# Another order of the attention's events in a fused attention, soft-MoE and MLP kernel

## The chip, the cores and the metric

The kernel runs on one core of one Trainium2 chip. Its time is the device time of one execution in microseconds (us). Five engines work side by side, each through its own list of instructions and strictly in the order of that list: TensorE (PE, with its weight loads as PEld), VectorE (DVE), ScalarE (ACT), GpSimd (POOL) and SyncE (SP), which in this kernel issues every DMA. An instruction that needs a result of another engine waits at the head of its list, and everything behind it waits too.

## The reference, cut to what matters

```python
def _attn_ref(q, k, v, g_q, g_k):             # q, k, v: (4, 12, 448, 64), float32
    def rmsnorm(x, g):
        rms = np.sqrt(np.mean(x * x, axis=-1, keepdims=True) + 1e-06)
        return x / rms * g
    q_n, k_n = (rmsnorm(q, g_q), rmsnorm(k, g_k))
    scores = np.matmul(q_n, k_n.transpose(0, 1, 3, 2)) / np.sqrt(64)
    scores = scores - np.max(scores, axis=-1, keepdims=True)
    attn = np.exp(scores)
    attn = attn / (np.sum(attn, axis=-1, keepdims=True) + 1e-09)
    return np.matmul(attn, v).astype(np.float32)

def _moe_ref(x, phi, w1, w2):                 # x: (1792, 768), 8 experts of 4 slots
    logits = x @ phi
    d = softmax(logits, axis=0);  slot_input = d.T @ x
    slot_out[e] = np.maximum(slot_input[e] @ w1[e], 0.0) @ w2[e]
    c = softmax(logits, axis=1);  return c @ slot_out

def _moe2_ref(x, w_in, w_out, alpha):         # d_model 768, d_ff 2048
    h = x @ w_in
    g = np.maximum(h, 0.0) + alpha * np.minimum(h, 0.0)
    return g @ w_out
```

The three follow each other. (The two softmax lines of the soft-MoE are shortened; a softmax there subtracts the maximum and divides by the sum plus 1e-9.) `w_in` and `w_out` arrive as float64 and are narrowed to float32 on the chip.

## The kernel before

**The attention.** The 48 heads are taken in 24 pairs of two heads; a pair has 2 x 448 = 896 rows, seven tiles of 128. Two pairs form a group, which is loaded together (`load_qk`, eight DMAs, L605 and L611; `load_v`, L601 and L611). A pair goes through these steps:

- ScalarE squares q and k (`norm_sum`, L641), VectorE sums the squares (L643); for a group, `norm_rs` makes the factors 1/rms (L653 to L663).
- GpSimd multiplies (L684), ScalarE and GpSimd split into a high and a low half in fp16 (L690, L697), TensorE transposes (`turn`, L710), ScalarE copies the result into the tiles q and k (`turned`, L717) and SyncE copies halves of them into the tiles kB and qB (L719, L721) and within q (`twin`, L726).
- TensorE computes rough scores (`rowmax_mm`, L760), VectorE takes their row maxima (`rowmax`, L769), TensorE transposes these (`turn_m`, L731), ScalarE copies them into `mr` (L737), and SyncE puts `mr` into a row of qB (L738).
- TensorE computes the scores exactly in two passes over the same PSUM bank (`score_mm`, L778): q times k, and then kB times qB. The second pass brings the missing products and, through the row that came from `mr`, the subtraction of the row maximum. So this pass cannot start before the DMA of L738 has landed.
- ScalarE takes the exponential (`score`, L792 to L799), VectorE or GpSimd makes its low half (`score_lo`, L810), TensorE multiplies by v (`av`, eight groups to a pair, L827 and L837), and VectorE divides by the sum (`av_out`, L852 to L865).

Between these steps run three background queues: `bg`, the soft-MoE's logits and its two softmaxes, batch by batch (L899 to L1011); `pf`, which fetches w_in and the first expert weights in pieces (`fetch_in`, L488, 512 KB; `fetch` with a cut of 6, L479, 256 KB); and `cv`, which narrows w_in (L502 to L514).

PSUM has two banks for exact scores (`psn`), three for rough ones (`psr`), one for the product with v (`psv`) and two for transposes (`pst`).

**What sets the order.** `plan` lists 2374 such events, each a function and its arguments. The table `ORDER` names them in the order in which they are called, and since scheduling is manual, each engine gets its instructions in just this order. Table `T` gives positions that build the list and settings that choose engines; it is the same in both kernels. SyncE's DMAs take eight semaphores in turn, so that each also waits for the DMA eight places before it.

**Behind the attention.** When the last pair's tiles are free, three rings of buffers open (`close_norm`, `close_score`, `close_exp`) and take expert weights: 11 units of 1.5 MB in all, six of them in pieces. The last batch's dispatch softmax follows, the experts (L1285 to L1314), for which each unit's buffer is filled again as soon as TensorE has read it, and then the two products of the MLP (L1459 to L1461), blocked over tokens. The load of alpha (L1195) stands in SyncE's list behind the eleventh unit and ahead of the twelfth; its buffer is free once the last batch's combine weights (L1011) are done. None of this is ordered by the table.

```python
        assert sorted(ORDER) == list(range(len(plan)))
        plan = [plan[i] for i in ORDER]
        ...
        for _, f, args in plan:
            f(*args)
            while waiting and waiting[0][1]():
                waiting.pop(0)[0]()
```

Of the kernel before, what the change touches and what calls it, by code (L numbers as in the profile page):

```python
# [232 lines left out]
    1775, 968, 992, 1076, 920, 969, 993, 1016, 932, 1028, 1040, 1052, 1064, 1100, 1148, 1124, 921, 1796, 970, 994,  # L233
    1172, 1797, 971, 995, 1196, 1244, 1220, 1077, 1101, 840, 850, 860, 870, 880, 890, 1268, 900, 910, 944, 1292, 1316,
    72, 192, 1149, 1125, 312, 96, 432, 1017, 216, 336, 552, 456, 1986, 2171, 576, 672, 696, 1173, 956, 933, 2172, 792,
    1340, 1798, 1197, 1245, 1029, 1041, 1269, 1221, 1293, 1053, 1065, 1317, 1078, 1102, 1126, 816, 1364, 1150, 1198,
    73, 193, 313, 97, 217, 337, 1246, 1174, 1222, 433, 1079, 1388, 457, 553, 577, 673, 1270, 1294, 945, 972, 996, 793,
    1127, 697, 817, 1341, 1318, 1103, 74, 1175, 973, 1151, 1365, 1412, 1413, 2173, 2174, 1389, 1799, 194, 841, 997,
    851, 1223, 314, 861, 871, 881, 891, 98, 218, 1018, 1030, 1800, 0, 24, 2175, 1987, 120, 1042, 1054, 1066, 1199,
    144, 168, 1801, 1080, 338, 1104, 1128, 901, 911, 240, 1247, 1295, 264, 288, 1152, 360, 384, 1436, 408, 1176, 48,  # L240
    957, 1776, 1988, 2176, 434, 554, 1200, 480, 674, 458, 578, 698, 1989, 1224, 600, 794, 504, 624, 528, 1802, 1803,
    720, 744, 648, 1508, 768, 1081, 1342, 1105, 1319, 1437, 1580, 1778, 1271, 2177, 1, 1556, 2178, 121, 1532, 25, 145,
    75, 818, 1366, 195, 1390, 99, 219, 169, 241, 265, 2179, 1804, 2180, 315, 1628, 1990, 1652, 1676, 435, 2181, 974,
    1991, 1129, 1805, 1153, 361, 385, 409, 339, 998, 975, 1604, 1700, 1724, 1248, 555, 675, 842, 852, 862, 872, 882,
    289, 892, 481, 49, 902, 459, 912, 505, 601, 529, 1992, 1748, 1177, 1225, 625, 1806, 2182, 1201, 1807, 1296, 579,
    1993, 721, 745, 649, 769, 795, 1343, 1509, 1994, 1995, 1581, 1272, 1320, 1808, 2183, 2184, 2, 26, 2185, 699, 819,
    1533, 122, 1809, 1810, 999, 1460, 1414, 1438, 146, 1811, 1812, 1813, 1629, 1082, 1996, 1997, 1814, 170, 1019,
    1031, 1043, 2186, 242, 2187, 1055, 1067, 2188, 50, 266, 1815, 1653, 1367, 1391, 1677, 1816, 1817, 362, 1557, 1605,
    922, 1484, 934, 1106, 1130, 290, 76, 386, 410, 1998, 482, 602, 1701, 1725, 1749, 1154, 196, 316, 100, 220, 946,
    506, 626, 976, 958, 1249, 722, 746, 340, 1297, 1321, 650, 530, 436, 2189, 460, 556, 1818, 580, 2190, 770, 1273,  # L250
    2191, 676, 1510, 1202, 796, 1178, 1226, 1083, 1558, 700, 820, 3, 1461, 1819, 1415, 1000, 27, 2192, 77, 197, 977,
    101, 221, 317, 341, 1630, 1792, 123, 243, 147, 1107, 843, 267, 51, 853, 1534, 1001, 1777, 1131, 171, 1368, 1344,
    291, 1820, 1392, 2193, 863, 1821, 1155, 1822, 437, 1582, 1439, 873, 883, 893, 1654, 903, 913, 2194, 1606, 2195,
    363, 387, 1678, 483, 1702, 1726, 1823, 1824, 1825, 1485, 461, 1826, 1250, 1750, 603, 557, 677, 507, 531, 1416,
    2196, 627, 723, 747, 1274, 1020, 1440, 1827, 1298, 581, 651, 701, 411, 771, 1511, 1322, 1999, 1559, 797, 1583,
    1203, 4, 28, 821, 2000, 2001, 1032, 1044, 1631, 1056, 1068, 1179, 124, 1828, 78, 198, 2197, 148, 102, 1535, 172,
    244, 1462, 2002, 2003, 1655, 268, 222, 318, 292, 2198, 52, 1679, 1227, 364, 978, 1084, 438, 1607, 923, 2199, 2200,
    2201, 1345, 388, 484, 508, 412, 558, 1780, 1829, 1486, 1830, 1831, 1108, 1703, 1727, 1832, 342, 1369, 1393, 604,
    724, 1132, 935, 2004, 628, 748, 1251, 1751, 532, 1299, 1323, 947, 772, 652, 1833, 1793, 678, 462, 582, 702, 1156,
    1512, 1204, 1275, 959, 1560, 1536, 1417, 798, 1002, 1584, 5, 2202, 1632, 29, 1180, 2005, 1441, 1834, 822, 53, 125,  # L260
    149, 2203, 79, 245, 1463, 1346, 979, 173, 199, 319, 269, 1487, 1228, 1085, 1109, 844, 103, 854, 223, 1608, 1656,
    343, 1680, 864, 1704, 1728, 2204, 293, 1779, 2205, 365, 439, 463, 389, 2206, 1157, 1835, 1370, 559, 1133, 2207,
    1836, 1837, 1205, 1394, 1752, 485, 509, 605, 629, 1181, 1003, 874, 884, 894, 1838, 904, 914, 1252, 1418, 653, 725,
    2208, 1276, 679, 799, 749, 2006, 1442, 1300, 413, 2209, 533, 1324, 773, 1513, 1585, 2007, 1561, 6, 126, 583, 703,
    823, 1464, 1839, 30, 1840, 150, 80, 1537, 2210, 246, 174, 270, 104, 200, 224, 54, 1229, 1609, 1086, 1347, 2211,
    2008, 2212, 366, 2009, 2010, 390, 1371, 1841, 1488, 1395, 414, 1842, 1633, 980, 2011, 320, 1657, 344, 294, 440,
# [1284 lines left out]
```

## Time and profile before

| what | us |
|---|---|
| median of 3 runs | 696.68 |
| the runs | 689.49 to 698.57 |
| the profiled execution | 698.2 |
| its span, first to last instruction | 696.2 |
| PE busy | 618.2 |
| DVE busy | 472.7 |
| ACT busy | 364.5 |
| POOL busy | 192.6 |
| mean granted TensorE clock | 0.967 |

The profile is of one execution. Busy time is the time in which an engine works on an instruction; the shares over the whole span are means over stages with different limits, so they are read stage by stage. In lists of waits, a wait for several results is put down to the one that came last by the profile, and that can be the wrong one where two land together. PSUM tiles carry the names psn, psr, psv and pst; DMA issues of SyncE are shown as SPq.

### The profile page before, as it was taken

What the parts mean: (1) busy time and instruction counts of PE and PEld (TensorE: products, weight loads), DVE (VectorE), ACT (ScalarE), POOL (GpSimd) and SP (SyncE); (2) the same over time, 40 slices, a digit from 0 to 9 for tenths busy, and PEclk for the clock granted to TensorE, in tenths of its full rate; (3) what the DMA queues carried; (4) which work ended last, traced back from release to release, by engine and by line L of the source; (5) the groups of instructions that cost most, each with busy time, mean ns of one, the idle gap of its engine ahead of it and who ended that gap; (6) DMA issues with size and microseconds to landing.
All of it is one profiled execution on the core that took longest, in us unless ns stands there. A gap on an engine that the chain in (4) does not pass through costs nothing.

```text
span 696.2 us, 14030 instructions
## 1 busy us (share of the span) xinstructions
PE 618.2 (89%) x5522; PEld 479.6 (69%) x5522; DVE 472.7 (68%) x967; ACT 364.5 (52%) x708; POOL 192.6 (28%) x200
## 2 busy tenths in 40 slices
PE   0799898898889999998998657899999999999997
PEld 0367665576656766775543213787899999999997
DVE  5788997899999999864311042999975545454541
ACT  2799996898898997772111121766531111111110
POOL 5976665466647654321101000000000000000000
PEclk9889999999999999998899979999999999999999
DMA  5477666644735622759799999250020101010101
GB/s 138 109 209 197 174 161 190 178 118 115 191 93 154 180 50 61 211 164 399 313 422 425 425 423 425 107 182 1 1 91 0 47 1 46 1 45 1 47 1 45
DMA packets 65425, 106.90 MB, mean 154 GB/s; under 512 B 34632, under 2 KB 51536, under 8 KB 61008
## 3 DMA queue, kind: packets, MB, share of 16 engines
q1 hardware_dynamic: 65360, 106.01, 45.6%
q8 instruction: 43, 0.70, 0.4%
q14 instruction: 22, 0.18, 0.1%
HBM read 92.18 MB, written 5.51 MB: 140 GB/s over the span
## 4 chain that ended last, share of the span: by engine, by line
PE 50%; DVE 23%; DMA 12%; ACT 8%; issue 3%; SPq 2%; POOL 2%; ACTq 0%; DVEq 0%; POOLq 0%
PE psa L1461 9%; PE psa L1460 9%; PE psa L1459 9%; DMA unit<-in_moe_w_dram 8%; DVE m L769 4%; PE psn L778 4%; PE psv L837 3%; PE psv L827 3%; PE psa L1285 2%; DVE e L810 2%; PE psr L760 2%; DVE wf L510 1%; ACT e L794 1%; PE psa L1314 1%; PE pst L1416 1%
## 5 line engine op out<-in xcount | busy, mean ns | idle before, releaser
L1459 PE MATMUL psa<-whi,gh 128*128 128x384 f32 (+1 forms) x448 | 152.7, 341 | 0.0
L1460 PE MATMUL psa<-wlo,gh 128*128 128x384 f32 (+1 forms) x448 | 151.8, 339 | 0.0
L1461 PE MATMUL psa<-whi,gl 128*128 128x384 f32 (+1 forms) x448 | 151.4, 338 | 0.0
L769 DVE TENSOR_REDUCE m<-psr 128x1 f16<-128x448 f32 x168 | 97.2, 615 | 5.9 <-PE psr L760 5.4
L1428 ACT CAST gh<-t 128x512 fp32r<-128x512 f32 x40 | 24.9, 622 | 123.0 <-DVE t L1425 122.5
L1461 PEld LDWEIGHTS psa<-whi,gl 128*128 128x128 f32 x448 | 84.7, 189 | 3.0 <-DVE gl L1408 0.2
L1460 PEld LDWEIGHTS psa<-wlo,gh 128*128 128x128 f32 x448 | 84.7, 189 | 2.8
L837 PE MATMUL psv<-vH,e 128*128 128x65 f16 (+1 forms) x1152 | 85.7, 195 | 1.0 <-DVE e L810 0.9
L1459 PEld LDWEIGHTS psa<-whi,gh 128*128 128x128 f32 x448 | 84.7, 189 | 2.6
L837 PEld LDWEIGHTS <-e 128*128 128x128 f16 (+1 forms) x1728 | 80.8, 106 | 1.5 <-DVE e L810 1.2
L1422 DVE TENSOR_SCALAR t<-pst,alpha_t 128x256 f32<-128x256 f32 x80 | 34.9, 476 | 61.9 <-PE pst L1416 61.9
L810 POOL TENSOR_TENSOR e<-ef,e 128x448 f16<-128x448 f32 x48 | 53.7, 1119 | 83.1 <-ACT ef L799 65.4
L827 PEld LDWEIGHTS psv<-vR,e 128*128 128x128 f32 (+1 forms) x384 | 59.6, 178 | 22.9 <-issue 10.9
L837 PE MATMUL psv<-vL,e 128*128 128x64 f16 (+1 forms) x576 | 73.7, 193 | 0.1
L794 ACT ACTIVATE e<-psn 128x448 f16<-128x448 f32 x120 | 65.1, 542 | 14.2 <-PE psn L778 11.1
L778 PE MATMUL psn<-q,k 128*128 128x448 f16 (+1 forms) x192 | 62.5, 368 | 11.0 <-DVE e L810 4.9
L827 PE MATMUL psv<-vR,e 128*128 128x65 f32 (+1 forms) x384 | 69.9, 264 | 1.9 <-DVE X L865 0.7
L760 PE MATMUL psr<-k,q 128*128 128x448 f16 (+1 forms) x192 | 58.8, 378 | 6.8 <-DVE m L769 4.0
L778 PE MATMUL psn<-qB,kB 67*128 67x448 f16 (+1 forms) x192 | 62.2, 364 | 2.8 <-DMA vR<-in_v_dram 2.8
L697 POOL TENSOR_TENSOR sp<-nf,sp 128x448 f16<-128x448 f32 x48 | 51.2, 1076 | 13.9 <-ACT sp L690 11.0
L810 DVE TENSOR_TENSOR e<-psn,e 128x448 f16<-128x448 f32 x72 | 44.2, 616 | 9.3 <-ACT psn L799 8.8
L710 PE MATMUL pst<-ident,sp 128*128 128x128 f16 x336 | 28.4, 233 | 19.2 <-POOL sp L697 19.0
(164 smaller groups left out, 1077.4 us busy)
## 6 DMA issues: line engine op xcount, KB each, us to landing
unit<-in_moe_w_dram SPq DMA_DIRECT2D x26, 1536.0 KB
unit<-in_moe_w_in_dram SPq DMA_DIRECT2D x24, 512.0 KB
rawo<-in_moe_w_out_dram SPq DMA_DIRECT2D x8, 1536.0 KB
unit<-in_moe_w_dram SPq DMA_DIRECT2D x36, 256.0 KB
out_dram<-osb SPq DMA_DIRECT2D x14, 384.0 KB
qk<-in_q_dram SPq DMA_DIRECT2D x24, 192.0 KB
qk<-in_k_dram SPq DMA_DIRECT2D x24, 192.0 KB
vR<-in_v_dram SPq DMA_DIRECT2D x48, 96.0 KB
```

The source lines that it names most:

```text
L697: eng.tensor_tensor(out=d["sp"][:, a, :, D:], in0=d["nf"][:, a], in1=d["sp"][:, a, :, 0:D], op=ALU.subtract)
L760: nc.tensor.matmul(pn[o0:o1, :S], d["q"][:, c0 : c0 + o1 - o0], d["k"][:, h * S : (h + 1) * S], start=True, stop=True)
L769: nc.vector.tensor_reduce(out=d["m"][:, c : c + 1], in_=d.pop(("pn", c))[:, :S], axis=AX.X, op=ALU.max)
L778: nc.tensor.matmul(pe[o0:o1, :S], lhs[:, c0 : c0 + o1 - o0], rhs[:, h * S : (h + 1) * S], start=st_, stop=not st_,)
L794: nc.scalar.activation(e2[:, 0], pe[:, :S], AF.Exp, scale=0.125)
L810: eng.tensor_tensor(out=e2[:, 1], in0=ef, in1=e2[:, 0], op=ALU.subtract)
L827: nc.tensor.matmul(pv[o0:o1, slot, :], d["e", c][:, qs], d["vv"][:, sl], start=(j == 0), stop=False,)
L837: nc.tensor.matmul(pv[o0:o1, slot, 0:wd], d["e", c][:, w // 2, qs], (vl if w == 1 else vh)[:, sl, 0:wd], start=(j == 0 and w == 0), stop=( ...
L1422: nc.vector.tensor_scalar(out=t0[:, cs], in0=ph[:, cs], scalar1=0.0, scalar2=alpha_t[:, f // 2, i : i + 1], op0=ALU.min, op1=ALU.mult)
L1459: nc.tensor.matmul(a, gh[f][:, ms], hi[:, hs], start=(f == 0 and not (packed and m % 2 == 1 and hf == 0)), stop=False)
L1460: nc.tensor.matmul(a, gh[f][:, ms], lo[:, hs], start=False, stop=False)
L1461: nc.tensor.matmul(a, gl[f][:, ms], hi[:, hs], start=False, stop=(f == KF - 1 and not (packed and m % 2 == 0 and hf == 1)))
```

## The change

The numbers of `ORDER` are replaced by another arrangement of the same 2374 numbers; they were searched for offline, with longer DMA times and random changes of the durations. Nothing else differs: each engine has the same instructions, tiles and engine choices. One line of the table before and after:

```diff
 ORDER = (
-    1775, 968, 992, 1076, 920, 969, 993, 1016, 932, 1028, 1040, 1052, 1064, 1100, 1148, 1124, 921, 1796, 970, 994,
+    1076, 968, 1775, 992, 969, 993, 1016, 921, 1028, 1040, 1052, 1064, 920, 1100, 1124, 1986, 1148, 1196, 1244, 2171,
 ...
```

**SyncE, between the scores of pair 6 and pair 7.** These are the loads of k for pairs 12 and 13 (qk), the copies of pair 8's halves (qB2, kB2), two pieces of w_in and of w1 (unit), and the row maxima of pair 7 (qB1<-mr). Before:

```order
L605 DMA qk_1531<-in_k_dram 128x2x192
L611 DMA qk_1531<-in_k_dram 64x2x64
L605 DMA qk_1531<-in_k_dram 128x2x192
L611 DMA qk_1531<-in_k_dram 64x2x64
L721 DMA qB2_118<-q_1641 64x896
L488 DMA unit_1493<-in_moe2_w_in_dram 128x1024
L719 DMA kB2_119<-k_1664 64x896
L488 DMA unit_1493<-in_moe2_w_in_dram 128x1024
L726 DMA q_1438<-q_1438 64x896
L479 DMA unit_1760<-in_moe_w1_dram 128x512 x3
L738 DMA qB1_116<-mr_1778 1x7x128
L479 DMA unit_1760<-in_moe_w1_dram 128x512
```

Now:

```order
L605 DMA qk_1525<-in_k_dram 128x2x192
L721 DMA qB2_118<-q_1648 64x896
L611 DMA qk_1525<-in_k_dram 64x2x64
L605 DMA qk_1525<-in_k_dram 128x2x192
L719 DMA kB2_119<-k_1670 64x896
L611 DMA qk_1525<-in_k_dram 64x2x64
L726 DMA q_1437<-q_1437 64x896
L488 DMA unit_1485<-in_moe2_w_in_dram 128x1024 x2
L738 DMA qB1_116<-mr_1784 1x7x128
L479 DMA unit_1814<-in_moe_w1_dram 128x512 x2
L601 DMA vR0_122<-in_v_dram 128x3x64 x2
```

The three pieces of w1 have moved from ahead of pair 7's row maxima to behind them, and the copies of pair 8 have moved in between the loads of k, so that the last load of k stands behind the copy of pair 8's k.

**ScalarE, from pair 8's k to the square of pair 12** (sqr reads what the loads above bring). Before:

```order
L717 COPY k_1664<-pst16_1654 128x896
L792 ACTIVATE e2_1714<-psn_1700 128x448
L794 ACTIVATE e2_1716<-psn_1703 128x448
L799 ACTIVATE psn_1703<-psn_1703 128x448
L502 ACTIVATE win0_1073<-unit_655 128x768
L794 ACTIVATE e2_1736<-psn_1732 128x448
L799 ACTIVATE psn_1732<-psn_1732 128x448
L794 ACTIVATE e2_1770<-psn_1763 128x448
L799 ACTIVATE ef_1772<-psn_1763 128x448
L883 COPY xT_1776<-pst_1709 128x448
L737 CAST mr_1778<-pst_1774 7x128
L641 ACTIVATE sqr_1793<-qk_1531 128x896
```

Now:

```order
L717 COPY k_1670<-pst16_1618 128x896
L792 ACTIVATE e2_1691<-psn_1688 128x448
L794 ACTIVATE e2_1719<-psn_1704 128x448
L799 ACTIVATE psn_1704<-psn_1704 128x448
L794 ACTIVATE e2_1722<-psn_1713 128x448
L799 ACTIVATE psn_1713<-psn_1713 128x448
L502 ACTIVATE win0_1089<-unit_783 128x768
L794 ACTIVATE e2_1751<-psn_1743 128x448
L799 ACTIVATE ef_1753<-psn_1743 128x448
L883 COPY xT_1762<-pst_1708 128x448
L737 CAST mr_1784<-pst_1738 7x128
L641 ACTIVATE sqr_1830<-qk_1525 128x896
```

The same ten kinds of instruction stand between the two ends; one narrowing step (L502) has moved back by two exponentials. What changed is that the square's load now follows the DMA that reads the k at the top.

**VectorE, at the start, from the second group's square sums to its factors** (u and y; m are row maxima of pair 0). Before:

```order
L643 TENSOR_REDUCE u_221<-sqr_222 128x2x7
L643 TENSOR_REDUCE u_221<-sqr_226 128x2x7
L769 TENSOR_REDUCE m_276<-psr_268 128x1
L769 TENSOR_REDUCE m_276<-psr_270 128x1
L769 TENSOR_REDUCE m_276<-psr_274 128x1
L769 TENSOR_REDUCE m_276<-psr_278 128x1
L769 TENSOR_REDUCE m_276<-psr_287 128x1
L769 TENSOR_REDUCE m_276<-psr_291 128x1
L656 TENSOR_SCALAR u_221<-u_221 128x28
L659 TENSOR_TENSOR t_282<-y_281 128x28
L661 TENSOR_TENSOR t_282<-t_282,u_221 128x28
L663 SCALAR_TENSOR_TENSOR y_281<-t_282,y_281 128x28
```

Now:

```order
L643 TENSOR_REDUCE u_231<-sqr_232 128x2x7
L769 TENSOR_REDUCE m_257<-psr_252 128x1
L769 TENSOR_REDUCE m_257<-psr_254 128x1
L769 TENSOR_REDUCE m_257<-psr_263 128x1
L769 TENSOR_REDUCE m_257<-psr_266 128x1
L643 TENSOR_REDUCE u_231<-sqr_270 128x2x7
L656 TENSOR_SCALAR u_231<-u_231 128x28
L659 TENSOR_TENSOR t_278<-y_277 128x28
L661 TENSOR_TENSOR t_278<-t_278,u_231 128x28
L663 SCALAR_TENSOR_TENSOR y_277<-t_278,y_277 128x28
```

Two row maxima have moved behind the factors, and one of the two square sums has moved behind four row maxima.

Behind the last rough-score matmul (L760) TensorE's list now holds 32 instead of 28 exact-score matmuls and 24 instead of 22 groups of the product with v.

## Rows read from the trace of the kernel before

**Rows 1.** The page's first line: the span and the number of instructions

```profile
span 696.2 us, 14030 instructions
```

**Rows 2.** Busy us (count) by engine in each stretch, granted clock, DMA share, GB/s

```profile
core 0: us, PE busy (x) PEld busy (x) DVE busy (x) ACT busy (x) POOL busy (x), PEclk, DMA share, GB/s
0.00:60.00 60.00, 36.69 (x338) 23.31 (x339) 42.83 (x104) 41.88 (x81) 43.94 (x54) 0.91 0.62 163
60.00:300.00 240.00, 218.06 (x2757) 159.70 (x2755) 226.90 (x471) 208.62 (x425) 137.32 (x129) 0.98 0.54 144
300.00:322.00 22.00, 21.19 (x310) 16.92 (x308) 11.10 (x31) 14.22 (x32) 4.17 (x5) 1.00 0.76 265
322.00:337.00 15.00, 12.38 (x94) 8.16 (x95) 7.09 (x25) 1.39 (x5) 0.91 (x2) 0.66 0.85 356
337.00:440.00 103.00, 78.16 (x600) 31.67 (x591) 25.46 (x68) 22.96 (x42) 6.27 (x13) 0.95 0.95 398
440.00:696.30 256.30, 251.73 (x1440) 239.82 (x1438) 159.36 (x273) 75.47 (x127) 0.00 (x0) 0.99 0.11 41
```

**Rows 3.** SyncE's queue: waiter, releaser, us in total, times, longest

```profile
SPq L1195 <- DVE cN L1011: 15.4, 1, 15.4
```

**Rows 4.** VectorE's waits from 60 to 300 us, largest first

```profile
DVE e L810 <- ACT psn L799: 5.0, 7, 1.8
DVE m L769 <- PE psr L760: 1.5, 1, 1.5
DVE z L852 <- PE psv L837: 1.3, 1, 1.3
```

**Rows 5.** TensorE in order of time: start us, us, form [idle before, releaser]

```profile
107.98 0.35 PE L778 MATMUL psn<-q,k 128*128 128x448 f16 x1 [0.43 <-ACT ef L799]
111.11 0.46 PE L778 MATMUL psn<-qB,kB 67*128 67x448 f16 x1 [2.79 <-DMA vR<-in_v_dram]
```

**Rows 6.** SyncE's DMA issues in order of time, in front of the pause

```profile
102.92 1.56 SPq L479 DMA_DIRECT2D unit<-in_moe_w_dram  x3
104.57 0.80 SPq L738 DMA_DIRECT2D qB<-mr  x1
```

**Rows 7.** Three short stretches with half clock, columns as in rows 2

```profile
110.00:116.00 6.00, 4.89 (x53) 4.51 (x54) 2.88 (x5) 1.91 (x5) 4.52 (x6) 0.72 0.77 208
132.00:140.00 8.00, 6.68 (x79) 3.88 (x79) 6.37 (x19) 4.80 (x11) 2.97 (x4) 0.79 0.40 90
268.00:276.00 8.00, 6.51 (x63) 3.96 (x62) 6.59 (x15) 5.30 (x12) 2.99 (x3) 0.79 0.03 7
```

**Rows 8.** VectorE in order of time, behind the pause

```profile
113.77 0.63 DVE L769 TENSOR_REDUCE m<-psr 128x1 f16<-128x448 f32 x1 [1.52 <-PE psr L760]
116.17 0.62 DVE L810 TENSOR_TENSOR e<-psn,e 128x448 f16<-128x448 f32 x1 [1.77 <-ACT psn L799]
```

**Rows 9.** The chain that ended last, 102 to 112 us: start us, us, what

```profile
103.00 0.37 PE psv L827 x2
103.37 0.27 PE psv L837 x9
104.99 0.87 PE psn L778 x4
```

**Rows 10.** ScalarE in order of time: pair 8's k, squares of pairs 12 and 16

```profile
98.91 0.88 ACT L717 COPY k<-pst 128x896 f16<-128x896 f16 x1
104.33 0.94 ACT L641 ACTIVATE sqr<-qk 128x896 f32<-128x896 f32 x1
158.18 0.95 ACT L641 ACTIVATE sqr<-qk 128x896 f32<-128x896 f32 x1 [2.01 <-DMA qk<-in_k_dram]
```

**Rows 11.** SyncE's issue of pair 16's last load

```profile
153.23 0.60 SPq L611 DMA_DIRECT2D qk<-in_k_dram  x1
```

**Rows 12.** The stretch of pair 16's wait, columns as in rows 2

```profile
155.00:160.00 5.00, 5.00 (x89) 4.38 (x88) 4.93 (x15) 2.99 (x7) 1.12 (x1) 1.00 0.83 247
```

**Rows 13.** GpSimd in order of time at the start

```profile
25.79 0.94 POOL L684 TENSOR_TENSOR nf<-qk,y 128x448 f32<-128x448 f32 x1 [0.65 <-DVE y L663]
```

232 rows, old and new, of the table ORDER are left out of this document.

## The prediction

> **What bounds the kernel now.** I read the stretches first, then the waits inside the stretch that an order can touch, then single rows around the longest of them. The attention's events fill the time up to about 322 us; behind them stand the soft-MoE's closing steps (to 337 us), the expert weights (to 440 us) and the two large matrix products (to the end) [rows 2]. The last two are 359 of the 696 us and their instructions stand in the same order in both kernels, so they can only start earlier or later. From 337 us the DMA engines are busy 95% of the time, at 398 GB/s [rows 2]. SyncE sat 15.4 us in front of the alpha load, until VectorE had finished the last batch's combine weights, and every expert fetch past the eleventh stands behind that load [rows 3]. So whatever the attention saves or loses reaches the end one for one: there is no slack behind it, and no more bandwidth to catch up with.
>
> Inside the attention VectorE is the bound from 60 to 300 us: busy 226.9 of 240 us [rows 2]. Its work does not change, so an order can win there only what is idle, 13.1 us. The three largest named waits are 7.8 us of that [rows 4]; the rest is gaps of a fraction of a microsecond between instructions. From 300 to 322 us TensorE takes over as the bound, 21.19 of 22 us [rows 2]. Before 60 us VectorE is idle for 17 us [rows 2], much of it before the first pair is normalized.
>
> **The longest pause.** TensorE began the first product of pair 7 at 107.98 us and could begin the pass that adds the row maxima only at 111.11 us, 2.79 us after it was ready [rows 5]. The page names a load of v, which that matmul does not read; the row maxima (qB<-mr) are what it needs, and they had been issued at 104.57 us [rows 6]. So a transfer of 1.8 KB took 6.5 us. Ahead of it, in the eight preceding transfers of SyncE's queue (no more are under way, since each waits for the one eight places before it), stood three copies of 112 KB, two pieces of w_in of 512 KB and three pieces of w1 of 256 KB (partitions by elements by bytes in the printed order): 2128 KB. The clock was then granted at half speed for part of 110 to 116 us (0.72 in the mean), and VectorE did 2.88 us of work in those 6 [rows 7]: its two waits there are 1.52 and 1.77 us, together 3.3 us [rows 8]. Two other places show the half clock, 132 to 140 and 268 to 276 us, with 1.6 and 1.4 us of VectorE idle [rows 7]; no transfer is waited for there.
>
> The Trainium skill, "DMA: Bandwidth & Descriptors", Specifications, gives about 0.6 us to the first byte for transfers issued from SyncE. By that figure alone 1.8 KB would have been there long before 108 us, another producer would be to blame, and the sum below would stay at 696.7 us (the first rival) instead of 693.4; the 6.5 us contradict it for a queue with work ahead, and I go by the row.
>
> **The change, part by part.** All instructions stay and only their order differs, so every cost is a wait made or lost.
>
> 1. *Pair 7's row maxima.* In the new order the three w1 pieces stand behind this transfer, and of the eight before it there remain 2 x 512, 3 x 112, 192 and 2 x 32 KB: 1616 KB. At the measured rate that is 6.5 x 1616 / 2128 = 5.0 us, so it lands at about 109.5 us on the clock of the old trace. TensorE comes to it later, too: between the small transpose of the maxima and the first use stand 11 instead of 7 score matmuls and 40 instead of 30 of the products with v. Four score matmuls took 0.87 us, one group of ten with v 0.37 + 0.27 us [rows 9]: 1.5 us more, so the need moves from 108.3 to 109.8 us. Landing and need now meet with 0.3 us to spare, and I take the pause as gone: **-3.3 us**. If the rate is no better than that, and the need does not move, 1.2 of the 2.79 us remain and the gain is 1.9 us; if the load is not the cause, it is 0.
>
> 2. *The loads of q and k for pairs 12 and 13, in the same burst.* Before, all eight stood together ahead of the copies of pair 8. Now the two copies (L721, L719) stand among them, and the last piece of k must wait in SyncE until ScalarE has made pair 8's k. In the old trace ScalarE ended that copy at 99.8 us and began the square of pair 12 at 104.33 us, 4.5 us later [rows 10], with ten instructions between; the new order has the same ten kinds there. The last piece needs SyncE's issue of the k copy first (about 0.55 us) and its own flight; for the one load that was waited for (pair 16, issued at 153.23, in at 158.18 us) the flight was 5.0 us [rows 10, 11]. That makes 5.5 us against 4.5: a new pause of ScalarE of about 1 us, between 0 (a short queue) and 2.6 us (the 6.5 us of part 1). The old pause of 2.01 us in front of pair 16's square goes, since its load now stands further ahead of it. VectorE was busy 4.93 of 5 us during that old pause [rows 12], so I cost both at **0**; what covers them is work queued for VectorE, and without it the new one would cost what part 1's pause cost, up to 3.3 us.
>
> 3. *The start.* VectorE makes the second group's factors after four row maxima, where it made them after six. But the last square sum of that group moves behind those four, so the factors come out at nearly the same time. GpSimd waited 0.65 us for them [rows 13]; it is what sets the pace there, in the same order before and after. **0**, between -0.65 and +0.65 us.
>
> 4. *The hand-over to the tail.* Behind the last row-maximum matmul stand 32 instead of 28 score matmuls and 24 instead of 22 groups with v. By part 1's durations that is 0.87 + 2 x 0.64 = 2.1 us more at the end, but TensorE has done that much less before, and its total is the same. **0**, at worst +2.1 us. The other row-maxima transfers keep distances like those that caused no wait.
>
> **Sum.** The profiled execution took 698.2 us (span 696.2 [rows 1]); minus 3.3 makes 694.9. It lies 1.5 us above the median of the runs shown (696.7), so against that median I say **693.4 us**, which is 0.5% less. A measurement of this kernel can tell about 2% from no change; its own runs lie between 689.5 and 698.6 us.
>
> **Rivals.**
> - *Hidden anyway (0.22).* The pause of part 1 vanishes, but VectorE stands idle a little later, or the time comes back when TensorE takes over at about 280 us. For it: TensorE, too, works 218 of 240 us [rows 2], and the tail holds 2.1 us more. Against it: VectorE's work is what the chain follows at 110 us. Time: 696.7 us. The same comes out if the load in the queue is not what held the row maxima up.
> - *The whole stretch runs evenly (0.15).* All named waits go, not only those behind transfers: 7.8 us [rows 4], and up to the 13.1 us. For it: two of the three half-clock stretches follow chance coincidences that a different order need not repeat. Against it: every tight order makes its own. Time: 696.7 - 7.8 = 689 us, at most 683.6.
> - *The wait moves onto ScalarE (0.18), slower than before.* The last piece of k for pair 12 now hangs on pair 8's k copy. If its flight is the 6.5 us of the same burst, ScalarE stands for 2.6 us with all later exponentials behind it; TensorE, which has two score banks, stops, falls to half clock as at 110 us, and VectorE loses 3.3 us as it did there. It decides from a flight of about 5 us on. With part 1 missing its gain as well and the tail's 2.1 us: 696.7 + 3.3 + 2.1 = 702 us. If several bursts do the same, 3.3 us each.
> - The forecast itself: 0.45.
>
> The range runs from 684 us (the even stretch at its best) to 704 us (the moved wait, and part of a second). Over 2% faster means below 682.7 us, more than all idle time of VectorE from 60 to 300 us and the run's offset together: 0.05. Over 2% slower means above 710.6 us, four or more new pauses of 3.3 us; the new order touches every burst, so I give 0.08 of the moved wait's 0.18 to that. Within 2%: 0.87.
>
> **What would show it.** Right: no wait of over 1 us for qB<-mr or a load between 100 and 120 us, full clock there, VectorE busy above 5.5 of 6 us; the second and third half-clock stretches may come back elsewhere. The alpha load is released about 3 us earlier than at 337 us, and all behind it is as long as before. Part 2 right: a pause of about 1 us in front of the square of pair 12, with VectorE busy through it. Wrong: a pause of several us on ScalarE there or a fourth stretch of half clock before 300 us; and wrong in kind if the stretch behind 337 us changes its length, since nothing in it was moved.

## The result and the profile after

The changed kernel took **703.3 us** (median of 4 runs, 700.4 to 706.4) against 697.6 us of the kernel before in the same comparison: a ratio of 1.0113 with a 95% interval of 1.0066 to 1.016. Six later runs gave 703.5 us and 1.0105 (1.006 to 1.015). It is about 1.1% slower; the forecast was 693.4 us.

The profiled execution took 700.4 us. Its stretches, with the columns of [rows 2]:

```profile
0.00:60.00 60.00, 34.11 (x323) 22.05 (x323) 43.63 (x102) 41.20 (x79) 43.47 (x53) 0.94 0.58 153
60.00:300.00 240.00, 216.29 (x2771) 160.39 (x2768) 232.68 (x474) 209.06 (x425) 137.92 (x128) 0.99 0.53 146
300.00:322.00 22.00, 20.99 (x309) 16.21 (x306) 11.69 (x31) 14.83 (x33) 5.17 (x5) 1.00 0.73 243
322.00:337.00 15.00, 11.58 (x95) 7.25 (x97) 7.64 (x26) 1.77 (x5) 1.41 (x2) 0.81 0.92 389
337.00:440.00 103.00, 78.73 (x590) 30.50 (x583) 22.82 (x64) 21.60 (x40) 5.76 (x13) 0.91 0.96 398
440.00:698.30 258.30, 253.87 (x1449) 242.19 (x1448) 161.48 (x276) 76.77 (x129) 0.00 (x0) 0.99 0.11 40
```

VectorE's waits from 60 to 300 us, which answer to [rows 4], then two of the three stretches of [rows 7] (columns as there):

```profile
DVE e L810 <- ACT psn L799: 0.9, 2, 0.5
DVE m L769 <- PE psr L760: 0.5, 2, 0.3
DVE z L852 <- PE psv L837: 0.4, 2, 0.3
```

```profile
110.00:116.00 6.00, 5.29 (x67) 3.54 (x64) 5.78 (x16) 5.57 (x13) 3.21 (x5) 1.00 0.68 208
268.00:276.00 8.00, 7.58 (x105) 5.86 (x102) 7.78 (x17) 5.28 (x12) 3.44 (x4) 1.00 0.33 101
```

What the prediction wanted to see is there. The same three waits are 1.8 us instead of 7.8, the clock is full, and VectorE is busy 5.78 of the 6 us that had the pause. But VectorE was busy 232.68 us of the 240 instead of 226.9 and got through hardly more by it, 474 instructions instead of 471. Over the whole program the same 967 instructions kept it busy for 479.9 us, where they had taken 472.7. The changed kernel's page:

```profile
PE 615.6 (88%) x5522; PEld 478.6 (69%) x5522; DVE 479.9 (69%) x967; ACT 365.2 (52%) x708; POOL 193.7 (28%) x200
```

Where these microseconds are shows in the groups of VectorE's lines from 60 to 338 us (count, then busy us and mean ns of one). Before:

```profile
L769 DVE TENSOR_REDUCE m<-psr 128x1 f16<-128x448 f32 x140 | 81.1, 614 | 2.0 <-PE psr L760 1.5
L643 DVE TENSOR_REDUCE u<-sqr 128x14 f32<-128x896 f32 x16 | 17.2, 1076 | 0.1
L510 DVE SCALAR_TENSOR_TENSOR win<-unit,win 128x768 uint32<-128x768 uint32 x16 | 17.1, 1067 | 0.3
L514 DVE SCALAR_TENSOR_TENSOR win<-unit,win 128x768 uint32<-128x768 uint32 x16 | 16.4, 1025 | 0.2
L504 DVE TENSOR_SCALAR win<-win 128x768 f32<-128x768 f32 x16 | 8.9, 559 | 0.0
L506 DVE TENSOR_SCALAR win<-win 128x768 uint32<-128x768 uint32 x16 | 8.9, 558 | 0.4
```

After:

```profile
L769 DVE TENSOR_REDUCE m<-psr 128x1 f16<-128x448 f32 x137 | 79.1, 616 | 0.7 <-PE psr L760 0.5
L514 DVE SCALAR_TENSOR_TENSOR win<-unit,win 128x768 uint32<-128x768 uint32 x16 | 19.2, 1202 | 0.3
L643 DVE TENSOR_REDUCE u<-sqr 128x14 f32<-128x896 f32 x16 | 17.2, 1077 | 0.1
L510 DVE SCALAR_TENSOR_TENSOR win<-unit,win 128x768 uint32<-128x768 uint32 x16 | 16.9, 1059 | 0.3
L506 DVE TENSOR_SCALAR win<-win 128x768 uint32<-128x768 uint32 x16 | 10.8, 678 | 0.4
L504 DVE TENSOR_SCALAR win<-win 128x768 f32<-128x768 f32 x16 | 9.7, 607 | 0.2 <-ACT win L502 0.2
```

What reads PSUM (L769), and the reduction of the squares (L643), take the same time in both. The narrowing of w_in, which works on SBUF alone, takes 56.6 instead of 51.3 us. The mean hides two kinds, which the order of time on VectorE and GpSimd shows (start us, us). The changed kernel around 266 us, and in the last row an L514 that runs while GpSimd has nothing to do:

```profile
264.54 1.03 POOL L697 TENSOR_TENSOR sp<-nf,sp 128x448 f16<-128x448 f32 x1
264.76 0.62 DVE L769 TENSOR_REDUCE m<-psr 128x1 f16<-128x448 f32 x1
265.29 0.61 DVE L810 TENSOR_TENSOR e<-psn,e 128x448 f16<-128x448 f32 x1
265.64 1.14 POOL L684 TENSOR_TENSOR nf<-qk,G 128x448 f32<-128x448 f32 x1
265.82 1.78 DVE L514 SCALAR_TENSOR_TENSOR win<-unit,win 128x768 uint32<-128x768 uint32 x1
266.86 1.53 POOL L684 TENSOR_TENSOR nf<-nf,y 128x448 f32<-128x448 f32 x1
280.45 0.96 DVE L514 SCALAR_TENSOR_TENSOR win<-unit,win 128x768 uint32<-128x768 uint32 x1
```

L514 takes 0.96 us where it is free. Here it begins at 265.82, while GpSimd works until 266.78, and takes 0.82 us longer. GpSimd's next multiplication then begins beside it and takes 1.53 us instead of 0.94: each holds the other up, and whoever began first is not touched. L769 and L810 begin beside a running GpSimd instruction too and keep their times. I call such a VectorE instruction **held**: over 0.1 us longer than the median of its line and shape (of those with at least six), between 60 and 340 us. (The expectations written first used a wider count, 21 and 12 held instructions with 13.3 and 6.8 us.) In all traces of this study every one so long began while a GpSimd instruction ran. The old order has 10 with 5.5 us in all, the new one 18 with 11.4. The profile books a hold as busy time and not as a wait, which is why it stood in no row on which the prediction rests.

The Trainium skill has the rule, "SBUF — State Buffer", Who interferes with whom: VectorE instructions with two inputs in SBUF, or in a fast mode that uses two ports, share a pair of ports with GpSimd, the first to start has it for its whole length, the other stands, and `tensor_reduce` on trn2 never contends. The rows agree: L514, with two inputs in SBUF, takes 1.78 us held and 0.96 free; GpSimd's multiplication that begins behind it takes 1.53 instead of 0.94; the reduction L643 takes 1.072 us free and 1.077 us beside GpSimd in the old order's trace (means of 3 and 13). Which mode L504 and L506 run in stands in no row; they are held too. Read against the list of VectorE's instructions, it would have been a rival to the forecast.

### The profile page after: what moved, and what is told of

Same layout as the page of the kernel before. It is cut to its first block, busy times and chain, and to the rows that moved or that the text cites. A ratio compares the mean times of both kernels' runs of the same rounds, so it can differ in the third digit from the quotient of the medians.

```text
span 698.3 us, 14045 instructions
## 1 busy us (share of the span) xinstructions
PE 615.6 (88%) x5522; PEld 478.6 (69%) x5522; DVE 479.9 (69%) x967; ACT 365.2 (52%) x708; POOL 193.7 (28%) x200
## 4 chain that ended last, share of the span: by engine, by line
PE 46%; DVE 28%; DMA 14%; ACT 6%; issue 3%; POOL 2%; SPq 0%; ACTq 0%; DVEq 0%; POOLq 0%
DMA unit<-in_moe_w_dram 11%; PE psa L1461 9%; PE psa L1460 9%; PE psa L1459 9%; DVE m L769 6%; PE psn L778 3%; PE psv L837 3%; PE psv L827 3%; DVE e L810 3%; DVE win L514 2%; DVE u L643 2%; PE psr L760 1%; DMA qB<-q 1%; DVE wf L510 1%; PE pst L1416 1%
## 5 line engine op out<-in xcount | busy, mean ns | idle before, releaser
L1460 PE MATMUL psa<-wlo,gh 128*128 128x384 f32 (+1 forms) x448 | 151.7, 339 | 0.0
L769 DVE TENSOR_REDUCE m<-psr 128x1 f16<-128x448 f32 x168 | 97.0, 617 | 4.3 <-PE psr L760 4.0
L810 POOL TENSOR_TENSOR e<-ef,e 128x448 f16<-128x448 f32 x48 | 51.7, 1078 | 81.8 <-ACT ef L799 66.4
L794 ACT ACTIVATE e<-psn 128x448 f16<-128x448 f32 x120 | 64.8, 540 | 14.6 <-PE psn L778 11.4
L760 PE MATMUL psr<-k,q 128*128 128x448 f16 (+1 forms) x192 | 57.8, 376 | 13.7 <-DVE m L769 8.4
L778 PE MATMUL psn<-q,k 128*128 128x448 f16 (+1 forms) x192 | 60.5, 358 | 9.8 <-DVE e L810 6.1
L778 PE MATMUL psn<-qB,kB 67*128 67x448 f16 (+1 forms) x192 | 60.5, 356 | 0.0
L697 POOL TENSOR_TENSOR sp<-nf,sp 128x448 f16<-128x448 f32 x48 | 52.8, 1108 | 17.9 <-ACT sp L690 14.3
L810 DVE TENSOR_TENSOR e<-psn,e 128x448 f16<-128x448 f32 x72 | 44.4, 618 | 4.8 <-ACT psn L799 4.2
L1285 PE MATMUL psa<-unit,slT 128*32 128x512 f32 x192 | 35.0, 693 | 14.0 <-DMA unit<-in_moe_w_dram 13.2
```

What stands on the lines that cost most here:

```text
L697: eng.tensor_tensor(out=d["sp"][:, a, :, D:], in0=d["nf"][:, a], in1=d["sp"][:, a, :, 0:D], op=ALU.subtract)
L760: nc.tensor.matmul(pn[o0:o1, :S], d["q"][:, c0 : c0 + o1 - o0], d["k"][:, h * S : (h + 1) * S], start=True, stop=True)
L769: nc.vector.tensor_reduce(out=d["m"][:, c : c + 1], in_=d.pop(("pn", c))[:, :S], axis=AX.X, op=ALU.max)
L778: nc.tensor.matmul(pe[o0:o1, :S], lhs[:, c0 : c0 + o1 - o0], rhs[:, h * S : (h + 1) * S], start=st_, stop=not st_,)
L794: nc.scalar.activation(e2[:, 0], pe[:, :S], AF.Exp, scale=0.125)
L810: eng.tensor_tensor(out=e2[:, 1], in0=ef, in1=e2[:, 0], op=ALU.subtract)
```

## The experiments

Theory A: the held instructions eat what the shorter waits gave. Theory B: the new order's own waits, or the clock behind the attention, make the loss. Theory C: the difference is only the spread of the runs. Theory D came with the second traces: the stretch behind the attention goes with the order in which the attention ends. The kernel before had a median of 695.6 to 696.5 us in the four comparisons, with 23 to 29 runs in each.

**More traces of both orders** (no edit).

> The changed kernel once more, unaltered, for a second trace and more times. Theory A (held VectorE instructions): a VectorE instruction that works on SBUF alone, by the two-input or the scalar form, and starts while a GpSimd instruction runs, ends only after it; the trace of the changed order has 21 such instructions between 60 and 338 us, which took 13.3 us more than the free ones of their lines, the old order 12 with 6.8 us. Then this trace shows again about 20 held instructions with 11 to 15 us, VectorE busy 293 to 298 us before 337 us (before: 288), and a time of 700 to 706 us. Theory B (the order's own waits and the clock of the first experts): 700 to 706 us too, but the held time may be anything, and a half-clock stretch behind 335 us shows again. Theory C (spread of the runs): 697 to 700 us, no difference from the kernel before.

> The changed kernel once more, unaltered, for a third trace. So far the old order's three traces have the alpha load at 336.8, 329.5 and 335.0 us and 359.4, 360.8 and 360.5 us from it to the end; the changed order's two have 336.3 and 336.7 us and 362.0 and 366.5 us. Theory A (held instructions): the alpha load again at 336 to 337.5 us, the same 18 held instructions with 11 to 11.6 us. Theory D (the new order ends its attention in another phase of TensorE's clock, so that the stretch behind it is longer as a rule): 362 to 367 us behind the alpha load, with 27 us or more of half clock between 320 and 460 us, where the old order has 17 to 24. If the rest is chance: 359 to 361 us there.

> The same, a fourth trace: alpha load at 336 to 337.5 us with the 18 held instructions (theory A), 362 to 367 us behind it with 27 us or more of half clock (theory D), or 359 to 361 us (chance).

> The kernel before once more, unaltered, for a second trace of it. The two traces of the changed order agree in the attention within 0.4 us (alpha load released at 336.3 and 336.7 us, the same 18 held VectorE instructions) and differ by 4.5 us behind it. The profiled execution of the old order (698.2 us) lies in the upper third of its own times (median 695.6 us). Theory A with 'the pause was a rare one': in this trace pair 7's row maxima wait less than the 6.5 us, the alpha load is released at 332 to 335 us and the time is 693 to 696 us; the held time is again 5 to 7 us. Theory B: the attention ends at 336 to 337 us again, and what the old order is ahead lies behind it: 354 to 358 us from the alpha load to the end, where the changed order has 362 to 366.

> The same, a third trace: whichever of the two holds in the second trace of the old order holds here too, if it is the rule and not chance: alpha load at 332 to 335 us and 359 to 361 us behind it (theory A), or alpha load at 336 to 337 us and 354 to 358 us behind it (theory B).

Measured, with all other traces of the study. "Alpha" is the release of the alpha load, the attention's end in the prediction's terms; the two right columns are the stretch from the last fetch of expert weights to the first matmul with w_in, and the length of these 48 matmuls (L1354):

| trace | time us | held, us | alpha at | alpha to end | fetch to L1354 | L1354 |
|---|---|---|---|---|---|---|
| before | 698.2 | 10, 5.5 | 336.8 | 359.4 | 32.7 | 5.4 |
| old_2 | 692.3 | 7, 3.6 | 329.5 | 360.8 | 32.7 | 5.4 |
| old_3 | 697.4 | 10, 5.9 | 335.0 | 360.5 | 32.7 | 5.4 |
| after | 700.4 | 18, 11.4 | 336.3 | 362.0 | 32.7 | 5.4 |
| after_again | 705.3 | 18, 11.3 | 336.7 | 366.5 | 34.9 | 8.0 |
| new_3 | 703.6 | 18, 11.2 | 338.1 | 363.4 | 34.2 | 5.4 |
| new_4 | 706.8 | 18, 11.4 | 340.0 | 364.8 | 34.5 | 6.6 |
| after_redw | 694.8 | 4, 2.0 | 331.5 | 361.2 | 32.7 | 5.4 |
| before_redw | 696.7 | 4, 2.3 | 335.4 | 359.3 | 32.8 | 5.4 |
| after_shift | 695.5 | 9, 4.2 | 332.1 | 361.4 | 32.7 | 5.4 |
| before_pf | 694.3 | 9, 4.9 | 332.6 | 359.7 | 32.7 | 5.4 |
| pf_shift | 695.2 | 5, 2.7 | 333.6 | 359.7 | 32.7 | 5.4 |
| pf_shift2 | 698.3 | 4, 1.9 | 331.0 | 365.2 | 34.9 | 8.1 |
| first_old | 692.7 | 8, 4.1 | 331.4 | 359.4 | 32.9 | 5.4 |
| first_new | 709.6 | 19, 12.4 | 341.1 | 366.3 | 34.7 | 8.2 |

Theory C falls: the loss is there again with the same ratio. The held time is a property of the new order (11.2 to 11.4 us in four traces). The third and fourth trace of the new order end their attention later than expected (338.1 and 340.0 us, not 336 to 337.5); 2.1 of the 3.7 us to the first trace arise before 70 us. The attention of the old order is not a fixed number: 329.5 to 336.8 us, with 359 to 361 us behind it, so B's account of the two old traces falls. Theory A's figures for them (332 to 335 us, 5 to 7 us held) hold in old_3, while old_2 ends earlier with 3.6 us held. From the profiled execution to old_2 it gains in steps, the largest 1.6 us at the pause of [rows 8]; four others, together 2.7 us, are instructions that were held in the one (1.03 us for L663 at 76.8 us) and free in the other (0.19 us). The prediction was made from the slowest of three.

The means of these traces give the loss in two parts: alpha at 337.8 against 333.8 us, and from there 364.2 against 360.2 us. Of the latter 0.9 us is no loss: in all traces that begin with the new order the alpha load comes 1.3 us behind the experts' first matmul, in all others 2.2 us. Counted from that matmul, the attention is 4.9 us longer and the rest 3.1.

**Narrowing that cannot be held.** Reductions of about the same length take the place of the four VectorE instructions:

```diff
-        eng.tensor_scalar_max(...)                  # L504, 768 elements
-        nc.vector.tensor_scalar(...)                # L506
-        nc.vector.scalar_tensor_tensor(...)         # L510
-        nc.vector.scalar_tensor_tensor(...)         # L514
+        for n in (392, 400, 768, 768):
+            nc.vector.tensor_reduce(out=rdum[:, 0 : n // 8], in_=dst[:, 0:n]..., axis=AX.X, op=ALU.max)
```

> The changed order, with the four VectorE instructions of each narrowing step replaced by reductions over SBUF of the same length (392, 400, 768 and 768 elements, estimated at 0.55, 0.56, 0.95 and 0.95 us from the 1.08 us of 896 elements): w_in is not narrowed, so the hidden layer's weights are other numbers. In the traces the reduction of the squares takes 1.075 us free and 1.078 us beside a running GpSimd instruction, so a reduction is not held. Theory A: the narrowing's share of the held time (8.4 of 13.3 us) goes, VectorE is busy 286 to 290 us before 337 us, and the time falls by 4 to 8 us against the changed kernel, to 695 to 699 us. Theory B: nothing falls, 701 to 706 us. Theory C: 697 to 700 us.

> The old order with the same replacement (w_in is not narrowed). Theory A: its narrowing was held 3.2 of 6.8 us, so it gains 1 to 3 us, to 694.5 to 697 us, less than the changed order gains; with both freed the changed order is at most 2 us longer or up to 3 us shorter. Theory B: no gain, 697 to 698 us, and the changed order stays 4 to 7 us longer than the old one. Theory C: 697 to 698 us, and no difference between the two.

These two took 697.2 us each (ratios 1.0025 and 1.0016). Their edit reached the narrowing of w_out as well, behind the attention, which the expectations overlooked, so their times compare with each other alone, and show no difference between the orders. The attention shows the point: alpha at 328.6 and 329.2 us. Hence a second pair, with w_in's narrowing alone:

> The changed order with the narrowing of w_in alone made of reductions (w_in is not narrowed, so the hidden layer's weights are other numbers); w_out's narrowing, behind the attention, stays as it is, unlike in the first pair of such kernels. Theory A: the alpha load at 328 to 329 us as in that pair, and as the stretch behind it keeps its 362 to 366 us, a time of 693 to 697 us. Theory B: the stretch behind it grows by the 8 us that the attention gains (it is bound by something that does not start with the attention's end), 701 to 705 us.

> The old order with the narrowing of w_in alone made of reductions (w_in is not narrowed, so the hidden layer's weights are other numbers); against the changed order with the same edit (693.5 us, 691.0 to 695.4) it compares the two orders without the held narrowing instructions. Theory A: the old order gains its 2 to 3 us of held narrowing and some of the pause at 108 us, 691 to 694.5 us, and the two orders are within 2 us of each other. Theory B and D: the old order is 4 us or more faster than the changed one here as well, below 689.5 us. The prediction's steps, if they were right but for the held instructions: the changed order is ahead by about 3 us, so 696 to 697 us here.

The replaced lines in after_redw, same columns as above:

```profile
L525 DVE TENSOR_REDUCE rdum<-win 128x96 f32<-128x768 f32 x32 | 30.4, 949 | 0.6
L525 DVE TENSOR_REDUCE rdum<-win 128x50 f32<-128x400 f32 x16 | 9.1, 569 | 0.4
L525 DVE TENSOR_REDUCE rdum<-win 128x49 f32<-128x392 f32 x16 | 8.9, 555 | 0.5 <-ACT win L522 0.2
```

48.4 us instead of 56.6, and the changed order takes **693.5 us** (ratio to the kernel before 0.9955, 0.9934 to 0.9975): 9.9 us less than with its own narrowing. That is theory A's figure (693 to 697), against theory B's 701 to 705. The alpha load was not as early as expected (331.5, not 328 to 329 us). With the old order the same edit gives 696.1 us (0.9967, 0.9929 to 1.0005), above theory A's 691 to 694.5 and far from B's 689.5: it is the figure expected if the prediction's steps were right but for the holds. Its trace has alpha at 335.4 us, with 3.27 us of the pause at pair 7, where before_red has 1.05: single traces of one attention lie several us apart. The old order loses its lead; the medians put the new one 2.6 us ahead, near the forecast's 3.3, but the intervals overlap and the first pair has the orders level, so that much is not shown.

**Eight held instructions moved**, work and instructions unchanged. One of eight such lines of the table:

```diff
-    291, 1155, 1678, 483, 557, 461, 1825, 2194, 507, 531, 603, 411, 1702, 1726, 1750, 627, 2195, 677, 581, 797, 701,
+    291, 1155, 1678, 483, 557, 461, 1825, 2194, 507, 531, 603, 411, 1702, 1726, 1750, 627, 677, 581, 2195, 797, 701,
```

> The changed order with eight of the narrowing's instructions that are held in both of its traces moved by one to four VectorE instructions (seven later, one earlier), to where the trace shows GpSimd idle or nearly done; the work is the same. Theory A: these eight were held 0.40 to 0.94 us, 5.3 us together; if the instructions behind keep their places against GpSimd, the held time falls from 11.4 to 6 us, and as their shift deals the rest anew, to anything from 4 to 9; the alpha load is released earlier than 336.5 us by the held time that went, within 1 us, and the time falls by 2 to 7 us against the changed kernel, to 696 to 701 us. Theory B: no change, 702 to 705 us, with the alpha load at 336 to 337 us or the time behind it longer by what it came earlier.

696.8 us, ratio 1.0019 (0.9985 to 1.0052), an interval that does not touch that of the changed order (1.006 to 1.015). 9 held with 4.2 us instead of 18 with 11.4, alpha at 332.1 us. That is 4.4 us earlier than the 336.5 expected of the unmoved order, not the 7.2 us by which the held time fell, so that part of the expectation is missed (against the mean of the four traces, 337.8, it is 5.7). The narrowing's rows are again those of the old order:

```profile
L510 DVE SCALAR_TENSOR_TENSOR win<-unit,win 128x768 uint32<-128x768 uint32 x16 | 16.9, 1055 | 0.3
L514 DVE SCALAR_TENSOR_TENSOR win<-unit,win 128x768 uint32<-128x768 uint32 x16 | 16.4, 1026 | 0.2
L506 DVE TENSOR_SCALAR win<-win 128x768 uint32<-128x768 uint32 x16 | 9.0, 563 | 0.4
L504 DVE TENSOR_SCALAR win<-win 128x768 f32<-128x768 f32 x16 | 8.9, 555 | 0.2 <-ACT win L502 0.2
```

Eight instructions, moved by one to four places in VectorE's list, give back 6.7 us of median. This is the strongest evidence for theory A, since nothing is left out and the lists of all other engines are the same.

**Part 1 of the prediction alone.** In the old order the three w1 pieces go behind pair 7's row maxima:

```diff
-    2008, 2212, 366, 2009, 2010, 390, 1371, 1841, 1488, 1395, 414, 1842, 1633, 980, 2011, 320, 1657, 344, 294, 440,
+    2212, 366, 390, 1371, 1841, 1488, 1395, 2008, 2009, 2010, 414, 1842, 1633, 980, 2011, 320, 1657, 344, 294, 440,
```

> Part 1 of the prediction alone: the old order with only the three w1 pieces between the last load and pair 7's row maxima moved behind these row maxima. The prediction's price: the 6.5 us wait falls under 3 us, the pause of TensorE and the half clock at 110 to 116 us go, -3.3 us against the kernel before (694.3 us). Rival 'hidden anyway' and theory B: 697 us, no difference. Theory A adds: what is won depends on how the instructions behind the pause now meet GpSimd; the held time (6.8 us before) may grow by some us and eat the gain, and the trace shows it as a longer VectorE busy time before 337 us.

The stretch of [rows 7] in this kernel:

```profile
110.00:116.00 6.00, 5.59 (x80) 4.54 (x81) 5.92 (x12) 5.57 (x13) 5.92 (x7) 1.00 0.88 248
```

VectorE 5.92 of 6 us and full clock: the pause is gone. This trace alone does not show that the w1 pieces were its cause, for the pause is not the same in each trace of the old order. In the unaltered old_2 and old_3 TensorE waits 0.67 and 0.12 us for these row maxima, and in old_3 before that 1.65 us for a copy of q that is issued ahead of the w1 pieces. In both, VectorE is down to 4.08 of 6 us right behind, with a granted clock of 0.72. The first row is old_2's, the second old_3's:

```profile
107.79 0.36 PE L778 MATMUL psn<-qB,kB 67*128 67x448 f16 x1 [0.67 <-DMA qB<-mr]
110.35 0.36 PE L778 MATMUL psn<-q,k 128*128 128x448 f16 x1 [1.65 <-DMA q<-q]
```

A longer stretch tells more: from the end of pair 5's last score matmul (pairs count from 0; the 96th of 384) to that of pair 9 (the 160th) the old order's three traces take 54.1, 52.0 and 52.8 us, before_pf 49.0, and two later kernels with the pieces in the same place 49.6 and 49.7. But before_red, with the pieces in their old place, is as short in its trace (49.5), while before_redw, with the same attention, takes 53.6. So the pieces are the likely cause of the pause and not a proven one. The time is 694.6 us, a ratio of 0.9979 (0.9951 to 1.0007): 1.5 us less, between 3.4 less and 0.5 more. The alpha load comes 4.2 us earlier than in the prediction's execution, but inside the range of the other two traces of the old order.

**A better version?**

> A version that may beat both: the old order with the three w1 pieces behind pair 7's row maxima, and three of its held VectorE instructions (0.72, 0.82 and 0.79 us in the trace of that kernel) moved by one to four VectorE instructions to where GpSimd is idle. Theory A: 2.3 us less held time if the rest keeps its place (the rest may be dealt anew by 1 to 2 us either way), so 691 to 694 us against 694.6 us of that kernel, a ratio to the kernel before of 0.992 to 0.998. Theory B and C: 694 to 696 us.

> The kernel with three held instructions moved (695.0 us, no faster than without the move) had its held time down from 4.9 to 2.7 us, but TensorE then waited 3.5 us at 183 to 187 us for pair 13's copy of q (112 KB), whose transfer was issued at 177.2 us behind three w_in pieces of 512 KB and the last loads of q and k. Here these three pieces go behind pair 13's row maxima, as the w1 pieces did at pair 7. Theory A with the prediction's part 1: that wait falls under 1 us and VectorE's 4.5 us with it, and the held time stays at 2 to 4 us, so 690 to 693 us, a ratio to the kernel before of 0.991 to 0.996. If the next transfer is late in its place (the load of v or pair 14's q) or the held time grows: 694 to 696 us.

The first (three events of before_pf moved) took 695.0 us, ratio 0.9979 (0.9947 to 1.0011): no gain, though the held time fell from 4.9 to 2.7 us. TensorE's list shows what came instead:

```profile
186.63 0.55 PE L778 MATMUL psn<-q,k 128*128 128x448 f16 x1 [3.50 <-DMA q<-q]
```

and SyncE's list what this copy stood behind:

```profile
174.19 0.54 SPq L488 DMA_DIRECT2D unit<-in_moe_w_in_dram  x1
174.83 0.52 SPq L719 DMA_DIRECT2D kB<-k  x1
175.44 0.55 SPq L721 DMA_DIRECT2D qB<-q  x1
176.04 1.07 SPq L488 DMA_DIRECT2D unit<-in_moe_w_in_dram  x2
177.21 0.47 SPq L726 DMA_DIRECT2D q<-q  x1
```

112 KB took over 9 us behind three pieces of 512 KB, the same pattern as in [rows 6]. With these pieces moved behind pair 13's row maxima (three numbers of the table) that wait is gone, the held time is 1.9 us and alpha is at 331.0 us, the earliest of these three; the median is 694.3 us, ratio 0.9976 (0.9941 to 1.0012). Theory A's figures for the two, 691 to 694 and 690 to 693 us, are missed. A gain of some tenths of a percent over the kernel before may be there, but is not shown.

**Half of each order**, cut at pair 12's first row maximum (the rest of the events follow in the other kernel's order):

> The changed order up to pair 12's first row maximum (about 150 us), and from there the old one. Theory A (held instructions): the new order's held ones up to 150 us (7 of 18, 5.2 us together) stay, so 100 us into the kernel it is as late as the new order (the 96th of the scores' matmul groups at 100 to 102 us, where the old order has 94 to 97), and what follows has the old order's held ones, 2 to 4 us; the attention ends 0 to 2 us before the new order's, and the time is 697 to 703 us. Theory D (the stretch behind the attention goes with the order of the attention's end): from the alpha load to the end 359 to 361 us, as in the old order. If that stretch goes with something else: 362 to 366 us here.

> The reverse: the old order up to pair 12's first row maximum, then the changed one. Theory A: the first half is the old order's (96th group at 94 to 97 us, the pause at 108 us with it), the second half has the new order's 11 held instructions (6.2 us) if they keep their place against GpSimd; the time is 695 to 701 us. Theory D: 362 to 366 us from the alpha load to the end, as in the new order, with 20 us or more of half clock between 390 and 450 us; else 359 to 361.5 us.

first_new took 703.7 us (1.0095, 1.0059 to 1.013), first_old 693.5 us (0.9963, 0.9925 to 1.0001). Both lie outside theory A's figures, the one just above, the other 1.5 us below. The loss is there with the new order's first half and not with its second. Theory A's count was half wrong: before 150 us the held time is as expected, 5.2 us in first_new and 0.5 in first_old, but behind it, where the halves have changed partners, 7.2 us fall to the old second half (3.0 to 3.9 behind its own first half), and 3.6 to the new one (6.2 behind its own). The held time of a stretch is thus not fixed by its order alone; what runs ahead of it shifts VectorE against GpSimd and deals it anew. Theory D falls: the stretch from alpha is 366.3 us with the old order's end (in a trace of 709.6 us, the slowest of that kernel's twelve runs), 359.4 with the new one's, and pf_shift2, which ends as the old order does, has 365.2.

## Why the prediction was wrong

- **The step that failed** is a half sentence of the part on the bound: VectorE's "work does not change, so an order can win there only what is idle". Its instructions do not change, the time they take did: 479.9 us instead of 472.7 over the program. In the two profiled executions the three waits of [rows 4] are 6.0 us shorter and the held time is 5.9 us longer, and the alpha load comes at 336.3 instead of 336.8 us: what the forecast counted as won was given back. In the four traces of the new order the held time is 11.3 us in the mean, against 5.0 in the three of the old one, and the attention, by the experts' first matmul, 4.9 us longer. after_shift and after_redw show it by intervention. The other 3.1 of the 8.0 us between the means are not explained by it (below); for them theory B's clock stays possible.
- **Part 1** came true at its place: the wait is gone, the clock full, and the stretch from the 96th to the 160th score matmul takes 48.9 to 49.0 us in the four traces of the new order, against 52.0 to 54.1. That the w1 pieces made the wait is likely, not proven. The 2.79 us of TensorE's wait on which the price rests are those of one execution; two others have 0.67 and 0.12. Alone it brings 1.5 us (3.4 less to 0.5 more), which is not shown to differ from none. In the new order it was more than used up ahead of that place, between 72 and 105 us, where seven held instructions cost 5.2 us (two with 1.6 us, or none, in the old order): the 96th score matmul ends at 100.3 to 102.8 us, against 94.1 to 97.2. At the 160th (149.2 to 151.7 against 146.1 to 150.2) much of that has been caught up.
- **Part 2**: no load is waited for by ScalarE between 60 and 300 us, so its price of 0 was right, and the pause of 1 us did not come as one: the square of pair 12 began 5.4 us behind the end of pair 8's k instead of 4.5, but ScalarE stood idle for none of it just before.
- **Part 3** (start, 0 within 0.65): the second pair's last score matmul ends at 52.0 to 53.1 us in the new order, 50.3 to 52.3 in the old, 1.2 us later in the means. The bound was probably too small, by less than 1 us; the two ranges overlap.
- **Part 4** (hand-over, 0): right; TensorE is busy 20.99 of the 22 us as in [rows 2].
- **The stretch behind 337 us as long as before**: not so, 3.1 us longer in the mean by the experts' first matmul. In after_again the 48 matmuls with w_in ran at 839 ns each, where the old order's trace has 594. Before, and in after_again:

```profile
L1354 PE MATMUL pst<-win,ST 128*32 128x512 f32 x48 | 5.4, 594 | 0.0
L1354 PE MATMUL pst<-win,ST 128*32 128x512 f32 x48 | 8.0, 839 | 0.0
```

  They fell into a half-clock stretch (granted clock 0.66 in the mean over them, against 1.00), which in the old order's traces ends before them. The table's right columns show it in five traces, three of the new order among them, and not in its first. By which rule a run gets it is **open**: it does not go with the order in which the attention ends (first_old, first_new, pf_shift2). Whether the new order meets it more often by its later time or four traces had bad luck is not told apart.
- **Rivals**: 'the wait moves onto ScalarE' came near the time (702 us), but by a mechanism that the trace does not show. 'Hidden anyway' had the kind right, time coming back a little later, without the place.
- **The base**: the execution stood 1.5 us above the three-run median, and 2.6 above the median of 29 runs (695.6).

No version here that still narrows w_in beats the kernel before by more than its interval; first_old comes nearest.

## What to carry to other kernels

Before an engine's work is called constant under a new order, split its lines by where they read, and look at the spread of one line's durations: a line whose instances take 0.96 or 1.8 us is held by something, and a longer busy time is a wait that the list of waits does not show. A search with fixed durations, even with random changes to them, cannot see such holds. Take two or three traces of a kernel before costing a pause that stands in one.

## What the runs showed of the hardware

- A VectorE instruction on SBUF (the two-input form, or a scalar form on float32 or uint32) that starts during a GpSimd instruction ends later by about what GpSimd had left, up to 0.94 us; the reductions (L643, L769) and the two-input form with one input in PSUM (L810) keep their medians to within 0.01 us.
- The new order's attention repeats its 18 held instructions in four traces nearly one for one (11.2 to 11.4 us), although their attention ends up to 3.7 us apart. The old order's three differ by 7.3 us at its end; 2.7 us of that are instructions held in one trace and free in another.
- The same 48 matmuls took 5.4 us at a granted clock of 1.00 (2.4 GHz) and 8.0 to 8.2 us where half clock (1.2 GHz) fell on most of them (0.65 to 0.66 in the mean).
